# Which 64 KB block of a head's K and V each SBUF partition receives, and how the load's source is written

## The chip, the core and the metric

One core of a Trainium2 chip runs the whole program. The core has compute engines with their own instruction queues (PE for matmuls, DVE for vector work, ACT for activations, POOL, and SP, which here only issues transfers) and 16 DMA engines that move data between the device memory (HBM) and the on-chip memory SBUF, which has 128 partitions. The metric is the device time of one execution in microseconds. The kernel before took 354.75 us (median of 3 runs, 354.65 to 355.23).

## The reference

One decoding step of a transformer block for a single token of width 512. A conditioning vector gives six modulation vectors; a layer norm and a projection give 32 query heads of 128; each group of four query heads attends to one of 8 cached key/value heads with 32,768 positions; then come the output projection, a residual, a second layer norm and a small feed-forward part.

```
mod = (silu(c) @ w_mod)                       # 512 x 3072
h = layernorm(x) * (1 + ca) + sa
q = h @ wq                                    # 32 heads of 128
scores = einsum(q, k_cache) * 128 ** -0.5     # 8 kv heads, 32768 positions each
p = softmax(scores)
o = einsum(p, v_cache)
x = x + ga * (o @ wo)
h = layernorm(x) * (1 + cb) + sb
x = x + gb * (relu(h @ w1) @ w2)
```

All arrays are bfloat16. One head's K is 32,768 x 128 x 2 bytes = 8 MB, and so is its V; the 8 heads make 134.2 MB, beside 15.2 MB of weights. The sum over positions doesn't depend on their order, as long as K and V of a head use the same one.

## The kernel before, in words

The kernel streams everything once. A head's K is seen as 128 blocks of 256 consecutive positions; a block is 64 KB of consecutive bytes (256 positions x 128 values x 2 bytes) and goes to one partition. The views `kv` and `vv` (L63, L64) say which: partition p receives block p, for K and V alike.

```
    kv = A_k_cache[0].rearrange("g (p j) d -> g p j d", p=P)
    vv = A_v_cache[0].rearrange("g (p j) d -> g p j d", p=P)
```

**Loads.** `load` (L108 on) makes one transfer out of a key such as `("k", g, steps)`: `steps` names quarters of the head, each with 64 positions per partition (`TK = 64`). A whole head in one transfer is 128 rows of 64 KB (8192 KB), two steps are 128 rows of 32 KB (4096 KB) with one row starting 64 KB after the other in HBM, and one step is 128 rows of 16 KB. The destination is a tile of the pool `ring`, which has three slots of 64 KB per partition. `stream_dma` (L140, L141) issues the transfer on SP's queue. Every large load of the program goes through this one line, in the order of the list `stream`: half of K of head 0, w_mod, wq, the other half, then K of head g+1 and V of head g in turn, for the first heads whole, for the later ones in halves, V of the last head as a half and two quarters, and at the end wo, w1 and w2. SP waits ahead of an issue until the slot to be filled has been read for the last time. The transfers that have been issued stand in line at the DMA engines.

**Compute.** For each head the DVE transposes K in place in 32x32 blocks (L426), PE forms the scores of all positions with four query heads (L445), the softmax follows with the exponential on ACT (L482), and PE multiplies the probabilities with V (L507), in hardware loops for the first heads. PE and DVE follow an order that is written out by hand (`manual_schedule`); K of head g+1 is turned and scored ahead of V of head g. Behind the last head come the projection with wo (L582 and its neighbours), the second layer norm, w1, w2 and one small store.

A transfer fills all its rows before its reader is released: a reader waits for the whole transfer, never for a row.

## Time and profile before

| what | value |
|---|---|
| median of 3 runs | 354.75 us |
| the profiled execution's own time | 354.43 us |
| its span from the first to the last instruction | 352.5 us |
| PE busy | 276.4 us (78%) |
| DVE busy | 200.9 us (57%) |
| HBM read | 149.42 MB, 424 GB/s over the span |
| mean granted clock of PE | 0.921 |

The profile's page lists busy times, then the span in 40 slices with the DMA engines' busy share and the GB/s that they moved, the DMA queues, the chain of work that ended last, the costliest groups of instructions and the transfers by line. A "packet" is one row's piece that one DMA engine moves. A second view, busy time by stretch, gives for any stretch of the span each engine's busy time, the granted clock, the DMA engines' mean busy share and the GB/s. A packet is counted where it ends or begins, so that short stretches can show a share a little over or under what was moved, and the ratio of GB/s to share is the steadier figure.

### The profile page before, as it was taken

To read this page: it belongs to the slowest core of one execution; us is meant where nothing else is said; L and a number is where in the kernel's file an instruction comes from. 1 tells how busy PE (TensorE), PEld (TensorE's weight loads), DVE (VectorE), ACT (ScalarE), POOL (GpSimd) and SP (SyncE) were. 2 spreads that over 40 slices of the span, in tenths; PEclk is the share of its full clock that TensorE was granted. 3 is DMA by queue.
4 is the path that set the end of the run, shared out by engine and by line. 5 is a ranking of instruction groups with operands and counts; after the bars stand their busy time and mean duration, and the time that the engine had idled before them with its cause. 6 is when DMAs were issued, how large, how long until landed. Compare 5 with 4: busy or idle time off the path is not lost. (4 is left out here: it accounts for less than half of the span.)

```text
span 352.5 us, 3650 instructions
## 1 busy us (share of the span) xinstructions
PE 276.4 (78%) x1285; PEld 112.7 (32%) x1285; DVE 200.9 (57%) x226; ACT 25.1 (7%) x69; POOL 3.1 (1%) x15
## 2 busy tenths in 40 slices
PE   0055891995998599976998499867999789989976
PEld 0021330341333233422433233322444334434433
DVE  6662464984079613974099506975684357744142
ACT  1200103002000200001000200011000100011000
POOL 2000000000000000000000000000000000000000
PEclk9996897698999969996999989996999999999986
DMA  8999989989999999899899899999999999999995
GB/s 353 404 436 440 496 372 469 461 379 469 431 409 455 424 424 461 387 448 469 387 454 469 387 455 461 396 402 450 435 422 424 450 429 420 433 454 403 429 413 217
DMA packets 5379, 149.58 MB, mean 424 GB/s; under 512 B 632, under 2 KB 888, under 8 KB 1784
## 3 DMA queue, kind: packets, MB, share of 16 engines
q1 hardware_dynamic: 5336, 149.43, 98.5%
q8 instruction: 8, 0.13, 0.1%
q14 instruction: 3, 0.02, 0.0%
q10 hardware_dynamic: 32, 0.00, 0.0%
HBM read 149.42 MB, written 0.00 MB: 424 GB/s over the span
## 5 line engine op out<-in xcount | busy, mean ns | idle before, releaser
L426 DVE STREAM_TRANSPOSE Ksb<-Ksb 128x2048 f32<-128x2048 f32 x60 | 133.1, 2275 | 59.6 <-DMA Ksb<-in_A_k_cache_dram 59.6
L507 PE MATMUL o_ps<-Vsb,P_g 128*16 (+1 forms) x512 | 126.6, 405 | 13.3 <-ACT P_g L482 10.0
L445 PE MATMUL S_ps<-Ksb,qbd 128*128 128x512 bf16 x512 | 120.8, 388 | 10.4 <-DVE Ksb L426 8.7
L445 PEld LDWEIGHTS <-qbd 128*128 128x128 bf16 x512 | 49.8, 99 | 77.7 <-issue 21.8
L507 PEld LDWEIGHTS o_ps<-Vsb,P_g 128*16 x352 | 33.6, 95 | 68.2 <-issue 38.3
L507 PEld LDWEIGHTS <-P_g 128*16 128x16 bf16 x160 | 13.8, 90 | 19.0 <-issue 0.4
L407 ACT COPY qbd<-qrep_sb 32x16 bf16<-32x16 bf16 x32 | 6.4, 201 | 175.2 <-PE S_ps L445 174.0
L487 DVE STREAM_TRANSPOSE P_g<-P_g 128x1024 bf16<-128x1024 bf16 x8 | 10.0, 1245 | 14.1 <-ACT P_g L482 14.1
L458 DVE TENSOR_REDUCE m_p<-S_ps 128x1 f32<-128x1024 f32 x7 | 8.6, 1223 | 12.7 <-PE S_ps L445 12.7
L309 PE MATMUL mod_ps<-wmq_sb,siluT 128*1 128x512 bf16 x24 | 3.6, 623 | 9.9 <-DMA wmq_sb<-in_w_mod_dram 9.9
L318 DVE STREAM_TRANSPOSE Ksb<-Ksb 128x2048 f32<-128x2048 f32 x4 | 8.9, 2280 | 1.7 <-DMA Ksb<-in_A_k_cache_dram 1.7
L463 PE MATMUL mT_ps<-ident_f,m_p 128*1 128x128 f32 x8 | 2.2, 270 | 8.9 <-DVE m_p L458 7.9
L482 ACT ACTIVATE P_g<-S_ps,nbias 128x1024 bf16<-128x1024 f32 x8 | 8.9, 1114 | 0.2
L493 PE MATMUL L_ps<-Lexp,ones_f 128*128 128x4 f32 x16 | 3.1, 263 | 6.4 <-DVE Lexp L490 4.3
L496 DVE RECIPROCAL Linv<-L_ps 128x4 f32<-128x4 f32 x8 | 1.3, 164 | 11.7 <-PE L_ps L493 11.7
L479 ACT ACTIVATE nbias<-Mb_ps 128x1 f32<-128x1 f32 x8 | 1.4, 171 | 88.1 <-PE Mb_ps L477 88.1
L542 PE MATMUL acc_ps<-mask_sb,Y 16*128 16x4 f32 x16 | 3.1, 258 | 5.5 <-DVE Y L538 5.5
L239 PE MATMUL xc_ps<-cx_sel,wmq_sb 16*128 16x2 bf16 x4 | 0.3, 172 | 8.8 <-DVE wmq_sb L233 8.8
L535 DVE TENSOR_TENSOR o_ps<-o_ps,smask 16x512 f32<-16x512 f32 x8 | 5.3, 668 | 2.8 <-PE o_ps L507 2.8
L573 DVE CAST o_sb<-o_ps 128x4 bf16<-128x4 f32 (+2 forms) x4 | 0.7, 166 | 9.9 <-PE o_ps L569 9.9
L493 PEld LDWEIGHTS L_ps<-Lexp,ones_f 128*128 128x128 f32 x16 | 2.6, 203 | 9.7 <-issue 6.4
L538 DVE TENSOR_REDUCE Y<-o_ps 16x128 f32<-16x512 f32 x8 | 5.4, 679 | 0.3
(116 smaller groups left out, 80.6 us busy)
## 6 DMA issues: line engine op xcount, KB each, us to landing
Ksb<-in_A_k_cache_dram SPq DMA_DIRECT2D x6, 4096.0 KB, 30.3
Vsb<-in_A_v_cache_dram SPq DMA_DIRECT2D x5, 4096.0 KB, 29.5
wmq_sb<-in_A_wq_dram SPq DMA_DIRECT2D x1, 4096.0 KB, 28.1
Vsb<-in_A_v_cache_dram SPq DMA_DIRECT2D x2, 2048.0 KB, 35.5
wmq_sb<-in_w_mod_dram SPq DMA_DIRECT2D x1, 3072.0 KB, 18.9
tail_sb<-in_A_wo_dram SPq DMA_DIRECT2D x1, 2048.0 KB, 22.7
tail_sb<-in_B_w_dram SPq DMA_DIRECT2D x1, 1344.0 KB
tail_sb<-in_A_wo_dram SPq DMA_DIRECT2D x1, 1024.0 KB, 24.8
```

The source lines that it names most:

```text
L309: nc.tensor.matmul(dst[j // 4][32 * (j % 4):32 * (j % 4) + 1, :], lhsT=src_T[:, kt:kt + 1], rhs=w[:, kt, j * 512:(j + 1) * 512], start=(kt ...
L318: nc.vector.transpose(out=t, in_=t)
L407: nc.scalar.copy(out=o, in_=i)
L426: t = nc.vector.transpose(out=KTt.bitcast(F32), in_=KTt.bitcast(F32))
L445: nc.tensor.matmul(S_ps_tiles[g], lhsT=qbd[g % 2][:, hp, 4 * (7 - s):4 * (7 - s) + P], rhs=KTv[:, 16 * sl:16 * sl + 16, h, :, par], start= ...
L458: behind_loop(nc.vector.reduce_max(out=m_p[:], in_=S_g.rearrange("p g f -> p (g f)"), axis=AX.X))
L482: nc.scalar.activation(out=P_g[:], in_=S_g.rearrange("p g f -> p (g f)"), func=ACT.Exp, bias=nbias[:], scale=scale, accum_out=l_g[:],)
L487: behind_loop(nc.vector.transpose(out=P_g[:], in_=P_g[:]))
L493: nc.tensor.matmul(L_ps[:], lhsT=ones_f[:], rhs=Lexp[:], start=True, stop=True)
L507: nc.tensor.matmul(o_tiles[g][:], lhsT=PT, rhs=Vx, start=False, stop=False, skip_group_check=True)
L535: nc.vector.tensor_tensor(out=o, in0=o, in1=smask[:].unsqueeze(2).to_broadcast([16, 4, Dh]), op=ALU.mult,)
L538: nc.vector.tensor_reduce(out=Y[:], in_=o.rearrange("p s d -> p d s"), op=ALU.add, axis=AX.X)
```

## The change

The views of K and V are cut in another way, and the load flattens each row. A head's 128 blocks are numbered by two indices, block = 16 i + e with e from 0 to 15 and i from 0 to 7, and the source is written with e outermost: 16 groups, 1 block apart, of 8 rows, 16 blocks (1 MB) apart, of consecutive bytes. The destination is as before: 128 partitions in order, each with one row. Read in order, the row (e, i) of the source goes to partition 8 e + i. So partition 8 e + i holds block 16 i + e, where it held block 8 e + i. K and V use the same order, the sizes of rows and transfers, their number, their order and every compute instruction stay as they are, and so do the loads of the weights.

```
-    kv = A_k_cache[0].rearrange("g (p j) d -> g p j d", p=P)
-    vv = A_v_cache[0].rearrange("g (p j) d -> g p j d", p=P)
+    kv = A_k_cache[0].rearrange("g (i e j) d -> g e i j d", e=16, i=8)
+    vv = A_v_cache[0].rearrange("g (i e j) d -> g e i j d", e=16, i=8)
...
             g, steps = key[1], key[2]
-            src = (kv if kind == "k" else vv)[g, :, TK * steps[0]:TK * (steps[-1] + 1), :]
+            src = (kv if kind == "k" else vv)[g, :, :, TK * steps[0]:TK * (steps[-1] + 1), :]
+            src = src.rearrange("e i j d -> e i (j d)")
             name = f"Ksb{g}" if kind == "k" else f"Vsb{g}"
             t = piece(name, TK * Dh * steps[0], TK * Dh * len(steps)).rearrange("p (j d) -> p j d", d=Dh)
```

## The prediction

> **What bounds the kernel now.** I read the page's first three parts, then the chain, then busy time by stretch, then the transfers and SP's waits.

> ```profile
> span 352.5 us, 3650 instructions
> ...
> PE 276.4 (78%) x1285; PEld 112.7 (32%) x1285; DVE 200.9 (57%) x226; ACT 25.1 (7%) x69; POOL 3.1 (1%) x15
> ...
> DMA  8999989989999999899899899999999999999995
> ...
> DMA packets 5379, 149.58 MB, mean 424 GB/s; under 512 B 632, under 2 KB 888, under 8 KB 1784
> ...
> q1 hardware_dynamic: 5336, 149.43, 98.5%
> ...
> DMA 10%; PE 5%; DVE 2%; issue 0%; SPq 0%
> DMA tail_sb<-in_A_wo_dram 7%; DMA tail_sb<-in_B_w_dram 3%; PE S_ps L445 3%; PE o_ps L507 2%; DVE Ksb L426 1%; PE end_ps L767 0%; DVE Y L538 0%; DVE o_ps L535 0%; PE acc_ps L542 0%; PE L_ps L493 0%; SPq L141 0%; DVE o_rows L772 0%; DVE o_bf L774 0%; DVE Linv L496 0%; PE o_ps L569 0%
> ```

> SP's queue keeps the 16 DMA engines occupied for 98.5% of the span, while PE has 78%. The chain covers only the last 17% and is mostly transfers, so it doesn't carry the argument. The stretches do:

> ```profile
> core 0: us, PE busy (x) PEld busy (x) DVE busy (x) ACT busy (x) POOL busy (x), PEclk, DMA share, GB/s
> 1.80:12.00 10.20, 0.85 (x6) 0.79 (x7) 6.25 (x30) 2.59 (x3) 1.35 (x5) 1.00 0.98 404
> 12.00:20.00 8.00, 0.00 (x0) 0.00 (x0) 7.14 (x4) 0.35 (x2) 0.00 (x0) 1.00 1.06 456
> 20.00:29.00 9.00, 5.68 (x34) 2.30 (x34) 4.55 (x13) 0.84 (x2) 0.00 (x0) 0.89 0.96 415
> 40.00:230.00 190.00, 155.96 (x642) 62.54 (x641) 117.50 (x90) 12.19 (x36) 0.00 (x0) 0.92 1.00 434
> 320.00:334.00 14.00, 14.00 (x67) 5.83 (x65) 2.98 (x8) 0.00 (x0) 0.00 (x0) 1.00 0.98 417
> 334.00:349.20 15.20, 12.44 (x139) 6.05 (x138) 5.45 (x22) 0.76 (x3) 0.00 (x0) 0.78 0.96 395
> ```

> From 40 to 230 us whole heads stream in 64 KB rows: share 1.00, 434 GB/s, so 434 / 16 = 27.1 GB/s per engine, or 65,536 B / 27.1 GB/s = 2.42 us per row. The stretches at 12 and 20 us are w_mod and wq, whose rows lie back to back in HBM and are 24 and 32 KB long (3 MB and 4 MB over 128 rows); GB/s over share is 430 and 432 there. The rate is one constant, whatever the row's length from 24 to 64 KB and whatever the distance between neighbouring rows. It is a fixed width, not HBM's mood, and every engine has all of it. PE is busy for 156.0 of 190 us: compute waits for data.

> ```profile
> Ksb<-in_A_k_cache_dram SPq DMA_DIRECT2D x6, 4096.0 KB, 30.3
> Vsb<-in_A_v_cache_dram SPq DMA_DIRECT2D x5, 4096.0 KB, 29.5
> ...
> Vsb<-in_A_v_cache_dram SPq DMA_DIRECT2D x2, 2048.0 KB, 35.5
> ...
> Ksb<-in_A_k_cache_dram SPq DMA_DIRECT2D x5, 35.9
> Vsb<-in_A_v_cache_dram SPq DMA_DIRECT2D x5, 38.4
> ```

> ```profile
> DVE Ksb L426 <- DMA Ksb<-in_A_k_cache_dram: 59.6, 8, 13.1
> ```

> The last two transfer rows are the ten whole heads (8192 KB each, by the kernel). K and V together are 10 x 8192 + 11 x 4096 + 2 x 2048 KB = 131,072 KB = 134.2 MB; at 433 GB/s (just under the 434 of the long stretch) that is 310 us of the 352.5.

> **The change, part by part.** *Instructions.* None is added or removed on any compute engine: zero. The order of positions is the same for K and V, and each reader waits for a whole transfer, so no new wait arises in the program. *Issues on SP.* 23 loads of K and V are described in another way, with 16 groups of 8 rows.

> ```profile
> L141 SPq DMA_DIRECT2D Ksb<-in_A_k_cache_dram x11: 327/328/532, 0.7 to 271.6; - x11
> ...
> SPq L141 <- PEq L512: 124.8, 6, 21.9
> SPq L141 <- DVE Ksb L426: 124.3, 8, 25.1
> ```

> If each issue takes 532 ns (the longest here) and not 328, SP spends 23 x 0.2 = 4.7 us more; SP's waits of 124.8 and 124.3 us hide it, except ahead of the very first load: at most 0.2 us. Behind SP's issues stand only other loads and the final store.

> *The reading side.* Sixteen engines read blocks 64 KB apart at one time and step by 1 MB. Each row stays 64, 32 or 16 KB of consecutive bytes. Bounds by rows: nothing to gain, because every engine already has its constant width; the price of a bad pattern is bounded by the slowest bulk stretch, 395 GB/s at 334 us (small rows): 134.2 MB at 395 is 340 us, so +30 us. I take 0, by the rows at 12, 20 and 40 us, which differ in spacing and not in rate. [...]

> *The writing side.* This decides. Today both sides of a load are 128 rows, and the hardware may deal them to 16 engines in any order that suits SBUF. After the change the source's outer count is 16 and the destination's is 128. The only cut into sixteenths that both descriptions have in common is one group e per engine: engine e writes partitions 8e to 8e+7 one after another. At row i, engines e and e+4 then write partitions 8e+i and 8e+32+i, always 32 apart. If partitions 32 apart hang on one entrance to SBUF as wide as one engine's stream, the pair shares 27.1 GB/s: a 64 KB row takes 4.84 us and not 2.42, and only half the entrances work at a time. No row of the trace shows such a meeting, so its cost is bounded by 0 (the constant is each engine's own width and the entrances are wider) and by the whole time of K and V once more, +310 us (the constant is the entrance's). I take the upper end, less a correction: the constant is the same to 1% at three row lengths and with all HBM patterns, which is what a port on the receiving side would give, and an in-step pair has nothing that parts it.

> [...]

> *The correction.* Pairs aren't started exactly together. The first stretch moved 404 where 433 would be full: 10.2 x (1 - 404/433) = 0.7 us is the most that the start is spread; I take 0.2 us between two of a pair. Each time that the leader passes to its next four partitions, the two are apart for that long. Whole heads have 10 x 2 such passages, halves and quarters 13 x 2, together 46 x 0.2 = 9 us, say 10.

> *The sum.* 354.4 + 310 - 10 = 654 us. It is made against the profiled execution (354.43, of which 352.5 is the span); the median of 354.75 lies 0.3 above, which is nothing here. What is late next: every transpose of K waits for its load (59.6 us now, up to 310 more); PE's 156 us of work per 190 us of stream fits twice into the doubled stretch, so nothing new becomes the bound. The weights' loads keep their form; w_mod only arrives later, behind the doubled first half (4 MB, 9.7 us more, inside the 310).

> **The rivals.** *The pairs fall out of step (slower, but far less).* If one of a pair gets more than half of the entrance, it moves ahead until it writes its second four partitions while the other writes its first, and they never meet again. For: nothing makes the shares exactly equal. Against: an even share keeps any lead as it is. Price: being four rows late once, 4 x 2.42 = 9.7 us. At the first half heads four rows take half as long, a lead of 9.7 us is then a whole round and the pair meets again: another 4.8 us if it parts again (369 us in all), or all halves and quarters doubled, 11 x 4096 + 2 x 2048 KB = 50.3 MB, 116 us (480 us). I take 400.

> *The cut stays as it is (not slower).* The hardware deals destination partitions as before and finds each one's source, or engines are not hindered by a shared entrance. Then only the reading side changes, which I priced at 0: 354.4 us. What decides is whether a 64 KB row still takes 2.42 us. For: the destination is unchanged and the 27.1 may be an engine's own width. Against: the two sides no longer have an outer count in common.

> *Reading costs something (slightly slower).* The cut stays, but 16 streams 64 KB apart get in each other's way in HBM: up to +30 us by the row at 334 us; half of that is 369 us.

> *Reading gains.* Neighbouring blocks are served faster. The most that a share of 1.00 leaves is the ends: 354.4 down to some 353.5. Against it stands the constant 27.1.

> **How the numbers follow.** Pairs meet throughout: 0.45 (own range 610 to 668 us: a larger correction of 50 us, and none, plus a few us of small costs). Pairs fall out of step: 0.19. The cut stays, no change: 0.21. Reading costs: 0.11. Reading gains: 0.04. About 0.2% is what a measurement can tell here, so slower has 0.45 + 0.19 + 0.11 = 0.75, same 0.21, faster 0.04. The prediction is the likeliest, 654. Since no single neighbour of it brings 8 in 10, the range runs from no change, 354, to 668; it leaves out the gain and the few per cent above.

> **What would show it.** If pairs meet: packets stay at 5379, the DMA share stays near 1.00 in the long stretch (a packet counts while it is held up) and GB/s there is about 217 and not 434; landings of whole heads go from 35.9 us to about 75; the weights' stretches keep 430 over share; DVE's wait at L426 grows by some 300 us. If pairs part: the slices show 217 only in the first one or two loads, and again where the halves begin. If the cut stays: 434 throughout. The prediction is wrong if a row of K keeps its 2.42 us.

## The result, and the profile after

The changed kernel takes 686.18 us (median of 6 runs, 679.55 to 688.75) where the kernel before takes 354.7 us (median of 6, 354.5 to 355.23): 1.931 times as long, with a 95% interval of 1.9215 to 1.9405. That is 331 us more. It lies 18 us above the upper end of the predicted range. The profiled execution took 679.55 us, its span 677.6 us.

The head of the page of the changed kernel, with the slices of the DMA engines' share and of the GB/s:

```profile
span 677.6 us, 3650 instructions
...
PE 306.4 (45%) x1285; PEld 121.0 (18%) x1285; DVE 201.0 (30%) x226; ACT 25.1 (4%) x69; POOL 3.1 (0%) x15
...
DMA  9999998999989989989999999998999999999997
GB/s 195 362 279 218 240 193 186 244 190 193 240 187 232 201 186 236 198 186 240 193 205 224 190 232 201 187 232 191 213 205 214 217 209 215 223 230 219 226 306 292
DMA packets 5379, 149.58 MB, mean 221 GB/s; under 512 B 632, under 2 KB 888, under 8 KB 1784
...
q1 hardware_dynamic: 5336, 149.43, 99.1%
```

The packets are the same in number, size and bytes, the engines are as occupied as before (99.1% beside 98.5%), and they move half as much (221 GB/s over the span beside 424). The two higher slices early hold w_mod and wq, whose loads weren't changed: from 28 to 37 us the stream runs at 431 GB/s, at a share of 1.00.

Busy time by stretch of the changed kernel (the last columns are granted clock, DMA share and GB/s):

```profile
40.00:230.00 190.00, 81.03 (x324) 31.41 (x324) 58.30 (x47) 9.87 (x32) 0.00 (x0) 0.69 1.01 210
230.00:440.00 210.00, 91.28 (x367) 36.22 (x365) 61.73 (x47) 4.36 (x14) 0.00 (x0) 0.72 1.00 207
440.00:640.00 200.00, 98.77 (x360) 37.98 (x359) 55.15 (x57) 6.22 (x14) 0.47 (x1) 0.74 1.00 215
```

210 and 207 GB/s stand where 434 stood. Per engine that is 13.1 and 12.9 GB/s: a row of 64 KB takes about 5.0 us and not 2.42. The trace also keeps the duration of each single row, which no view prints: the 1,280 rows of 64 KB take 2.42 us before and 5.09 us after (medians), and the shortest after takes 4.83. Who waits is what was expected; here are the transfers, DVE's wait and SP's issues:

```profile
Ksb<-in_A_k_cache_dram SPq DMA_DIRECT2D x5, 102.7
Vsb<-in_A_v_cache_dram SPq DMA_DIRECT2D x5, 101.5
```

```profile
DVE Ksb L427 <- DMA Ksb<-in_A_k_cache_dram: 349.1, 10, 55.1
```

```profile
L142 SPq DMA_DIRECT2D Vsb<-in_A_v_cache_dram x12: 536/537/600, 45.8 to 554.8; - x12
L142 SPq DMA_DIRECT2D Ksb<-in_A_k_cache_dram x11: 536/537/669, 0.7 to 516.1; - x11
```

DVE's wait for K grew from 59.6 to 349.1 us. Each issue of K and V costs SP 537 ns and not 328, which is hidden as before. The landing of a whole head takes 102.7 us, because a load is still issued as soon as its slot has been read: its own 8192 KB take 40 us at 210 GB/s, and for the rest of the time it stands behind one and a half others.

### The profile page after: what moved, and what is told of

Its sections match the earlier page's. It is cut to its first block, busy times and chain, and to the rows that moved or that the text cites. A ratio compares the mean times of both kernels' runs of the same rounds, so it can differ in the third digit from the quotient of the medians.

```text
span 677.6 us, 3650 instructions
## 1 busy us (share of the span) xinstructions
PE 306.4 (45%) x1285; PEld 121.0 (18%) x1285; DVE 201.0 (30%) x226; ACT 25.1 (4%) x69; POOL 3.1 (0%) x15
## 2 busy tenths in 40 slices
DMA packets 5379, 149.58 MB, mean 221 GB/s; under 512 B 632, under 2 KB 888, under 8 KB 1784
## 3 DMA queue, kind: packets, MB, share of 16 engines
q1 hardware_dynamic: 5336, 149.43, 99.1%
## 4 chain that ended last, share of the span: by engine, by line
another core or an unknown queue 55%; DVE 22%; PE 14%; DMA 6%; ACT 2%; issue 1%; SPq 0%; DVEq 0%; ACTq 0%
DVE Ksb L427 17%; PE S_ps L446 6%; PE o_ps L508 6%; DMA wmq_sb<-in_A_wq_dram 6%; ACT P_g L483 1%; DVE m_p L459 1%; DVE P_g L488 1%; DVE Y L539 1%; DVE o_ps L536 1%; PE q_ps L381 1%; PE end_ps L768 0%; DVE o_ps L528 0%; PE acc_ps L543 0%; PE hid_ps L745 0%
## 5 line engine op out<-in xcount | busy, mean ns | idle before, releaser
L427 DVE STREAM_TRANSPOSE Ksb<-Ksb 128x2048 f32<-128x2048 f32 x60 | 133.1, 2277 | 349.1 <-DMA Ksb<-in_A_k_cache_dram 349.1
L446 PE MATMUL S_ps<-Ksb,qbd 128*128 128x512 bf16 x512 | 137.8, 430 | 169.6 <-DVE Ksb L427 168.1
L508 PE MATMUL o_ps<-Vsb,P_g 128*16 (+1 forms) x512 | 139.0, 435 | 138.7 <-issue 104.6
L446 PEld LDWEIGHTS <-qbd 128*128 128x128 bf16 x512 | 53.6, 106 | 250.1 <-DVE Ksb L427 110.9
L508 PEld LDWEIGHTS <-P_g 128*16 128x16 bf16 x160 | 16.5, 105 | 61.6 <-issue 50.2
L467 DVE TENSOR_REDUCE Mrow<-mT_ps 1x4 f32<-1x128 f32 x8 | 2.2, 274 | 15.8 <-PE mT_ps L464 15.8
L381 PE MATMUL q_ps<-wmq_sb,hT 128*1 128x512 bf16 x32 | 3.4, 598 | 2.5 <-DMA wmq_sb<-in_A_wq_dram 2.5
## 6 DMA issues: line engine op xcount, KB each, us to landing
Ksb<-in_A_k_cache_dram SPq DMA_DIRECT2D x6, 4096.0 KB, 80.4
Vsb<-in_A_v_cache_dram SPq DMA_DIRECT2D x5, 4096.0 KB, 82.4
wmq_sb<-in_A_wq_dram SPq DMA_DIRECT2D x1, 4096.0 KB, 38.3
Vsb<-in_A_v_cache_dram SPq DMA_DIRECT2D x2, 2048.0 KB, 92.1
tail_sb<-in_A_wo_dram SPq DMA_DIRECT2D x1, 2048.0 KB, 47.8
```

The costliest lines, as they stand in the source:

```text
L381: nc.tensor.matmul(q_ps[i][32 * a:32 * a + 1, :].rearrange("o (h e) -> o h e", e=32), lhsT=hT[:, kt:kt + 1], rhs=wq_f[:, kt, i, a], start= ...
L427: t = nc.vector.transpose(out=KTt.bitcast(F32), in_=KTt.bitcast(F32))
L446: nc.tensor.matmul(S_ps_tiles[g], lhsT=qbd[g % 2][:, hp, 4 * (7 - s):4 * (7 - s) + P], rhs=KTv[:, 16 * sl:16 * sl + 16, h, :, par], start= ...
L508: nc.tensor.matmul(o_tiles[g][:], lhsT=PT, rhs=Vx, start=False, stop=False, skip_group_check=True)
```

## The experiments

Four theories were held against each other. **W**, the prediction's: the new source is cut so that one engine writes eight consecutive partitions, engines e and e+4 write 32 partitions apart in step, and partitions 32 apart share one entrance, so that the two that meet are slow. **R**: the new order of reads in HBM is slow. **D**: a source of three dimensions is slow in itself. **F**: an engine is slow when it writes partitions that the plain 128-row load gives to another engine. Two more, **C** and **S**, came up on the way.

**The old neighbourhoods, cut as after.**

```
-    kv = A_k_cache[0].rearrange("g (i e j) d -> g e i j d", e=16, i=8)
+    kv = A_k_cache[0].rearrange("g (e i j) d -> g e i j d", e=16, i=8)
...
+            (se, ne), (si, ni), row = src.ap
+            src = AP(src.tensor, src.offset + (ni - 1) * si, [[se, ne], [-si, ni], row])
```

(V likewise. The step backwards is only there to keep the source from being read as 128 equal rows.)

> K and V are again read in the old neighbourhoods (partition 8e+7-i gets... block 8e+7-i is read as row i of group e, so engine e reads the same eight neighbouring blocks as the natural order has), but the source is written as 16 groups of 8 rows with a step backwards, so that it can't be read as 128 equal rows. Every K and V byte is read once, K and V in the same order. Theory W (the cut into 16 groups makes two engines write through one entrance of SBUF, in step): as slow as the changed kernel, 675 to 690 us, about 210 GB/s in the long stretch. Theory R (reading blocks 64 KB apart with steps of 1 MB is slow in HBM): like the kernel before, 354 to 360 us and 434 GB/s. Theory D (a source of three dimensions is slow for the DMA engines in itself): 675 to 690 us, as W.

Measured: 686.64 us (680.06 to 688.04), 1.9276 times the kernel before (1.9174 to 1.9379). Its long stretch:

```profile
40.00:230.00 190.00, 77.45 (x315) 30.17 (x315) 58.30 (x47) 9.87 (x32) 0.00 (x0) 0.71 1.00 207
```

The whole loss is there without the new order of reads. R falls, W and D stand.

**Reads 64 KB apart, cut as before.**

```
+            src = src.rearrange("p j d -> p (j d)")
+            src = AP(src.tensor, src.offset, [[TK * Dh, P], src.ap[1]])
```

This kernel leaves out most of K and V: its rows overlap.

> The source stays 128 equal rows, but rows start 16 KB apart and overlap, so that rows four apart lie 64 KB apart and several engines read in neighbouring 64 KB; most of K and V isn't read, and parts are read up to four times. The same bytes per transfer, the same destination. Theory W: like the kernel before, 354 to 356 us, 434 GB/s. Theory R: clearly slower, as far as 686 us if 64 KB between neighbours is the cause. Theory D: 354 to 356 us.

Measured: 354.84 us, 0.9996 times the kernel before (0.9986 to 1.0005), and at full width:

```profile
40.00:230.00 190.00, 155.23 (x642) 62.24 (x641) 117.12 (x90) 12.18 (x36) 0.00 (x0) 0.92 1.00 432
```

R falls from this side too.

**Groups of four rows in place of eight.**

```
-    kv = A_k_cache[0].rearrange("g (i e j) d -> g e i j d", e=16, i=8)
+    kv = A_k_cache[0].rearrange("g (i e j) d -> g e i j d", e=32, i=4)
```

(V likewise.)

> The source is cut into 32 groups of 4 rows (block = 32 i + f, group f from 0 to 31, row i from 0 to 3, partition 4 f + i): again three dimensions that can't be read as 128 equal rows, again neighbouring groups 64 KB apart and rows 2 MB apart, every byte read once. What differs from the changed kernel is that a group is four partitions and not eight. Theory W (which partitions one engine writes decides): if the hardware can deal groups of four to engines as it deals single rows, 354 to 357 us and 434 GB/s. Theory D (a source of three dimensions is slow in itself): 675 to 690 us and 210 GB/s. Theory R (reads 64 KB apart) would also say 675 to 690, but the run with rows 16 KB apart already speaks against it.

Measured: 354.88 us, ratio 1.0 (0.9991 to 1.001).

```profile
40.00:230.00 190.00, 155.49 (x639) 62.31 (x638) 116.50 (x90) 12.19 (x36) 0.00 (x0) 0.92 1.00 431
```

D falls: three dimensions cost nothing here (431 GB/s beside 434), where a group is four partitions. That groups of four go to the engines as single rows do is inferred from the unchanged rate. The idea of the change, engines reading near each other, neither gains nor loses anything in this run, as the prediction priced it.

**The entrances, one row at a time.** Ahead of the kernel before, ten small loads five times over, each with rows of 64 KB, one per engine (eight per engine in the last), to chosen partitions. Between them stands a load of 128 short rows, which makes each wait for the one before. (In the code cuts from here on, words behind a # are the document's.)

```
+        quiet()
+        nc.sync.dma_start(out=onto(0, 4, 4), in_=some[0:4])     # first partition, count, step
```

> The kernel before, with small loads ahead of it, one after another, five times each, into the slot that K of head 1 fills later: rows of 64 KB, one per engine, to chosen partitions; each waits for the one before. The time from issue to landing of each form, beside a fixed part common to all. (1) partitions 0,1,2,3; (2) 0,4,8,12; (3) 16,20,24,28; (4) 0,8,16,24; (5) 0,32,64,96; (6) 0,4,...,28; (7) 0,8,...,56; (8) 0,8,...,120; (9) 0,4,...,60; (10) all 128. Theory W: a row takes 2.4 us where every engine has its own entrance, (2), (3), (4) and (6); 4.8 us where two meet, (5), (7), (8) and (9), so 2.4 us more than (2); 9.7 us for (1). Theory F: (3) and (4) are as slow as (7) though no two engines meet. Theory D says nothing here: all have two dimensions.

SP's lines for four probes of the fourth round, in order of time. L174 is the load between; the time from a probe's start to the start of the next L174 is its time from issue to landing, with a part common to all. The table has nine; the tenth, all 128 rows, took 21.67 us. Rounds two to five agree within 0.25 us, and the first is disturbed by the kernel's own first loads.

```profile
337.88 0.27 SPq L179 DMA_DIRECT2D Ksb<-in_A_k_cache_dram  x1
348.79 0.33 SPq L174 DMA_DIRECT2D Ksb<-in_A_k_cache_dram  x1
350.54 0.65 SPq L181 DMA_DIRECT2D Ksb<-in_A_k_cache_dram  x1
355.78 0.33 SPq L174 DMA_DIRECT2D Ksb<-in_A_k_cache_dram  x1
...
372.00 0.55 SPq L187 DMA_DIRECT2D Ksb<-in_A_k_cache_dram  x1
379.14 0.33 SPq L174 DMA_DIRECT2D Ksb<-in_A_k_cache_dram  x1
...
396.93 0.56 SPq L193 DMA_DIRECT2D Ksb<-in_A_k_cache_dram  x1
404.68 0.33 SPq L174 DMA_DIRECT2D Ksb<-in_A_k_cache_dram  x1
```

| line | partitions | us to landing |
|---|---|---|
| L179 | 0, 1, 2, 3 | 10.91 |
| L181 | 0, 4, 8, 12 | 5.24 |
| L183 | 16, 20, 24, 28 | 5.25 |
| L185 | 0, 8, 16, 24 | 5.24 |
| L187 | 0, 32, 64, 96 | 7.14 |
| L189 | 0, 4, ..., 28 | 5.08 |
| L191 | 0, 8, ..., 56 | 7.26 |
| L193 | 0, 8, ..., 120 | 7.75 |
| L195 | 0, 4, ..., 60 | 7.60 |

**Pairs shifted against each other.** If a meeting slows only its pair, shifting one of each pair by its four rows should end the loss in the whole heads. Three extra loads of 64 KB rows to partitions 0–11, 0–7 and 0–3 are meant to occupy the lower engines first (which engine serves which row isn't shown); the second kernel has rows of 32 KB.

```
+    late = NTILE * TK * Dh        # the second kernel: // 2
+    for k in (12, 8, 4):
+        nc.sync.dma_start(out=piece("Ksb1", 0, late)[0:k], in_=kv[0].rearrange("e i j d -> e i (j d)")[0:k, 0, 0:late])
```

> The changed kernel, with three small extra loads at the start: 64 KB rows to partitions 0 to 11, 0 to 7 and 0 to 3 of the slot that K of head 1 fills later. They occupy engines 0 to 11, 0 to 7 and 0 to 3, four engines on one entrance, so each takes about four rows' time (9.7 us) and engines 0-3 come to lag 4-7, and 8-11 to lag 12-15, by four rows of a whole head. Theory W: the pairs no longer meet in the whole heads (434 GB/s there, from about 60 us on), and meet again in the halves, where 9.7 us is a whole round (about 210 GB/s): some 510 us in all, 480 to 540. Theories R and D: nothing gained, 686 + 29 = 715 us, 210 GB/s in the whole heads.

> The same with extra loads of 32 KB rows, so that the lag is 4.85 us. Theory W, with a lag that stays as it is: in the whole heads a pair meets for half of the time (each four rows take 1.5 times as long, 275 to 290 GB/s), and in the halves, whose four rows take 4.85 us, the pairs no longer meet (434 GB/s): the reverse of the run with the full lag; some 475 us in all, 455 to 500. Theories R and D: 686 + 15 = 700 us, 210 GB/s throughout.

Measured: 694.67 us (2 runs, 692.04 to 697.29) and 703.14 us (2 runs). The whole heads of the first kernel and a stretch that has mostly its halves, then the whole heads of the second:

```profile
100.00:230.00 130.00, 53.34 (x207) 21.05 (x206) 43.08 (x31) 5.65 (x15) 0.00 (x0) 0.70 1.00 209
440.00:640.00 200.00, 104.06 (x383) 40.28 (x384) 67.82 (x59) 5.29 (x14) 0.47 (x1) 0.74 1.00 231
```

```profile
100.00:230.00 130.00, 52.56 (x200) 20.50 (x200) 44.05 (x33) 4.36 (x14) 0.00 (x0) 0.70 1.00 209
```

No gain in the whole heads, and none in the time, against what W expected. So W lacked something, or eight consecutive partitions per engine are slow for a reason of their own (theory S).

**A cut into seven consecutive partitions.** The order of the kernel before, with each load in two.

```
+            stream_dma(t[0:112], src[0:112])
+            stream_dma(t[112:P], src[112:P])
```

> The order of the kernel before, with two dimensions on both sides, but each load of K and V in two: partitions 0 to 111 and partitions 112 to 127. 112 isn't cut like 128: seven consecutive partitions per engine. If only two engines that stand on the same entrance at one moment slow each other (Theory W in the form of the prediction, entrances repeating after 32 partitions), few of the 112 rows meet: 7 rows of 2.42 us, and the 16 rows, four engines to an entrance, 9.7 us: 26.6 us per 8 MB and not 19.3, 310 us become some 430, in all 460 to 500 us. If any engine that writes other partitions than those dealt to it in the 128-row load is slow (Theory F, foreign entrances): 7 x 4.84 + 9.7 = 43.5 us per 8 MB, in all some 740 us. Theory D: as the first, 460 to 500 us.

Measured: 699.37 us (2 runs, 697.62 to 701.11); its long stretches:

```profile
40.00:230.00 190.00, 82.87 (x330) 32.30 (x323) 58.29 (x47) 9.87 (x32) 0.00 (x0) 0.69 1.01 215
230.00:440.00 210.00, 90.72 (x358) 35.67 (x357) 60.90 (x46) 4.36 (x14) 0.00 (x0) 0.71 1.01 213
440.00:640.00 200.00, 91.40 (x334) 34.93 (x333) 52.66 (x52) 5.36 (x14) 0.47 (x1) 0.71 0.99 200
```

Counted so, and if each engine takes seven consecutive partitions, the 16 engines stand on 14 or 15 different entrances at each row of the larger load, so only one or two pairs meet; still all of it runs at half pace (200 to 215 GB/s). With F unlikely after the probes, this and the two runs before suggest theory C: **a shared entrance sets the pace of all sixteen engines.** Taken strictly, C gives 7 x 4.84 + 9.7 = 43.5 us per 8 MB, or 193 GB/s, and W gives 26.6 us, or 315 GB/s; the 200 to 215 measured lie nearer to C, and the difference is open. By C the shifts of the two kernels before didn't become what was meant either. While the lower engines filled a crowded entrance, the leaders were held to the same pace, and their lead in the end was the bytes of one extra row (64 KB, one row and not four). Pairs one row apart still meet in three rows of four, and as the two sets of pairs are shifted by two rows against each other, there is no moment of the whole heads without a meeting. In the halves a lead of 64 KB is two rows: there all pairs are apart in two rows of four, and all meet in the other two. From 500 to 640 us the first kernel does move 238 to 242 GB/s, where the changed kernel has 218 and the second one 212. An estimate from the row times (1.21 us before, 2.56 us in the control below) would be 278, so C gives the direction of this gain and not its size. All of this was worked out after these runs.

**All pairs apart, or half of them.** Theory C says how to get rid of the loss: make leads in bytes, and for all pairs at once. Loads in halves throughout make four rows 128 KB; one extra load of 24 rows is meant to give engines 0–11 128 KB more, and two of 4 rows to give engines 0–3 another 128 KB.

```
-        stream += [("k", g + 1, s) for s in (halves if g >= HALVED else whole)] + [("v", g, s) for s in (halves if g >= HALVED else whole)]
+        stream += [("k", g + 1, s) for s in halves] + [("v", g, s) for s in halves]
...
+    later = piece("Ksb1", 0, NTILE * TK * Dh)
+    lp = later.ap[0][0]
+    extra = [(24, 0, 1), (4, 24, 4), (4, 25, 4)]      # rows, first partition, step; the second kernel: the first alone
+    for n, first, step in extra:
+        to = AP(later.tensor, later.offset + first * lp, [[step * lp, n], [1, NTILE * TK * Dh]])
+        nc.sync.dma_start(out=to, in_=A_k_cache[0, 0].rearrange("(p j) d -> p (j d)", p=P)[0:n])
```

> The changed kernel with all loads of K and V in halves (rows of 32 KB, so that four rows are 128 KB per engine), and three extra loads behind the first: 24 rows of 64 KB (engines 0 to 11, 128 KB each) and twice 4 rows of 64 KB (engines 0 to 3, 128 KB). Engines 12-15 then lead 8-11 by 128 KB, and 4-7 lead 0-3 by 128 KB: both sets of pairs are apart by exactly four rows. Theory C (one entrance that two engines share sets the pace of all sixteen, so only a schedule without any meeting is fast; bytes moved, not time, make a lead): no meeting is left in the halves, 400 to 434 GB/s in the long stretch, 375 to 430 us in all. Theory W in the form of the prediction (a pair's meeting slows that pair only): the same. Theory S (a load that is cut into eight consecutive partitions per engine is slow whatever the order in time): 690 to 705 us and 210 GB/s.

> The same with only the first extra load (24 rows, engines 0 to 11): engines 12-15 lead 8-11 by four rows, and 0-3 stay in step with 4-7. Theory C: the meetings that are left slow all sixteen engines, 210 GB/s at a DMA share of 1.00, 685 to 700 us, no gain from half of the meetings being gone. Theory W in the form of the prediction: engines 8 to 15 move their rows at full pace and stand idle until the others are done, so about the same time and GB/s, but a DMA share of about 0.75. Theory S: share 1.00, 690 us.

> The changed kernel with all loads of K and V in halves and no extra load: the control of the two others. All theories: as the changed kernel, 675 to 695 us, 205 to 217 GB/s.

Measured: all pairs apart 440.6 us (436.25 to 443.43), 1.2447 times the kernel before (1.2401 to 1.2493), above the 375 to 430 us expected; half of them apart 660.87 and 691.77 us (two executions); the control 676.77 us (2 runs), 1.9077 (1.9039 to 1.9116). Three stretches with all pairs apart:

```profile
120.00:180.00 60.00, 46.30 (x192) 18.08 (x191) 31.34 (x28) 4.36 (x14) 0.00 (x0) 0.91 1.00 406
180.00:240.00 60.00, 48.92 (x211) 20.26 (x209) 36.53 (x27) 2.60 (x10) 0.00 (x0) 0.89 1.01 401
360.00:420.00 60.00, 38.03 (x165) 14.65 (x163) 16.86 (x23) 2.66 (x4) 0.47 (x1) 0.83 0.99 293
```

and two with half of the pairs apart (of the execution of 691.77 us; the other left no trace):

```profile
120.00:230.00 110.00, 45.51 (x167) 17.46 (x165) 32.26 (x28) 4.36 (x14) 0.00 (x0) 0.69 1.00 210
230.00:440.00 210.00, 98.81 (x373) 38.10 (x374) 59.75 (x46) 4.36 (x14) 0.00 (x0) 0.74 1.01 212
```

and one of the control:

```profile
40.00:230.00 190.00, 85.43 (x325) 32.73 (x325) 58.52 (x47) 9.87 (x32) 0.00 (x0) 0.71 1.00 208
```

The same cut into eight consecutive partitions runs at 401 to 406 GB/s (208 in the control) with the extra loads that are to keep any two engines from one entrance at a time, so S falls, and with it F: the loads of K and V, and so the partitions that an engine writes, are those of the control. The stretch from 360 us has the two quarters of the last V, in whose shorter rows a lead of 128 KB is a whole round; there the rate drops again, as it should: two slices of the page, 10.9 us each, have 210 and 213 GB/s from 380 us on.

With half of the pairs apart the trace has the rate of the control, and the share is 1.00 and not 0.75. The single rows settle who is slow: from 60 to 440 us none of the 2,442 rows of 32 KB takes less than 2.16 us, and their median is 2.56, as in the control; with all pairs apart it is 1.27 (120 to 300 us), and before it was 1.21. If only the pairs that meet were slow, half of the rows would be near 1.21. So, if the first extra load parts the pairs that it is meant to part, the engines that meet nobody are as slow as the others. That is theory C, and it speaks against pairs that slow only themselves. By the same count four entrances are shared at every moment of this kernel; that a single one would do the same isn't shown. The two executions lie 5% apart: the shorter one is 16 us under the control and under the 685 to 700 that C expected, so a gain of some 2% from half of the pairs isn't excluded.

Of the 86 us by which the first kernel misses the kernel before, some 26 are lost ahead of 60 us, 9 from there to 120, 18 from 120 to 360 and 19 from 360 to 420 us (an estimate from each stretch's GB/s against 433). The 2.1 MB of the extra loads are another 5 us. The rest wasn't taken apart, nor why 401 to 406 GB/s aren't 434.

## Why the prediction was right or wrong

- **What bounds the kernel** held: DMA at a constant 27.1 GB/s per engine, and compute that waits. Nothing new became the bound.
- **The reading side at 0** held: ratios of 0.9996 and 1.0 with reads 64 KB apart, and the same time with the new order of reads (686.18 us) and the old one (686.64 us) under the same cut.
- **Issues on SP** held: 537 ns beside the 532 ns that the text took, all hidden.
- **The writing side**, the mechanism that decided, held: an engine's eight consecutive partitions, pairs 32 apart, one entrance for two. Where it fell short is in who is slowed: not only the pair, but all sixteen engines, as the run with half of the pairs apart indicates (no row of 32 KB under 2.16 us). In the changed kernel every pair meets, so rows come out about doubled either way (5.09 us beside 2.42). The run with the old read order shows that the cut alone brings the loss, the probes show the entrances, the groups of four show that the cut is what matters, and the run with all pairs apart that the meeting does it. That engine e gets exactly partitions 8e to 8e+7 is inferred from these, not read off a trace, and so are the engines that the extra loads occupy and the reason given for the dealing, the outer counts of 16 and 128.
- **Its size was wrong**, and with it the range: 686.18 us lies above 668. Two terms of the sum failed. The upper end of "+310 us, the whole time of K and V once more" was taken as a bound, but two engines on one entrance together move less than one alone: at 210.6 GB/s (the mean of the three stretches after, weighted by their length) K and V take 134.2 / 210.6 = 637 us, 327 more and not 310 (a row took 5.09 us, not 4.84). And **the correction of 10 us was worth nothing.** It let each pair gain from its own small offset, once for every four partitions, and no run shows such a gain: in the runs with shifted pairs (209 GB/s in the whole heads) a pair's offset is worth nothing, or next to nothing, while other pairs meet. That four neighbouring partitions share an entrance, which the correction and the rival below both count with, was an assumption that no row of the trace before shows; the probes show it for partitions 0 to 3 (10.91 us, where 0, 4, 8 and 12 took 5.24). With both terms put right, 354.4 + 327 = 681 us beside the 679.55 of the profiled execution, the shortest of the six. The 210.6 is read from that same execution, so the sum says that no third term is missing, and not why the rate is what it is.
- **The rival "pairs fall out of step"** rested on the same wrong step. Pairs can be out of step, as in the two runs with extra loads, and the loss stays whole in the whole heads; only when all are apart at once does most of it go.
- **What would show it:** the packets, the share, 217 GB/s (210 came) and DVE's wait (289.5 us more, some 300 said) were as told, and the weights kept their rate. The landing was not: 102.7 us, not 75. A whole head's own 19 us became 40, but its waiting in line grew from some 17 to some 63 us (the landing less its own time), since slots come free earlier against the slower stream.

## What to carry to other kernels

In these runs a load's rate hung on which partitions were written at one time. 128 rows against 128, and groups of four partitions, kept the full rate (434 and 431 GB/s); groups of eight cost a factor of 1.93 in time (210 GB/s) though every byte, row and packet was the same, and loads cut into 112 and 16 partitions were as slow (699.37 us). That the outermost counts of the two sides settle the dealing is the prediction's inference; only these forms were tried. The sign in this profile was a DMA share of 1.00 at half of the usual GB/s. Don't price a contended entrance only by the engines that stand on it: with half of the pairs apart the whole stream moved 210 GB/s here, as with none apart (208).

## What was not expected of the hardware

**Crowded entrances held up all sixteen engines.** With half of the pairs apart: 210 GB/s at share 1.00, and no row of 32 KB under 2.16 us; with all of them apart, 401 to 406 GB/s. How an engine that meets nobody comes to be held up isn't shown.

**Two on one entrance moved less than one alone, in a long stream.** If every pair meets after the change, eight entrances carry the 207 to 210 GB/s of the whole heads, 25.9 to 26.3 each, where one engine alone had 27.1 before (434 / 16). In the probes, with one row per engine, it isn't so: four rows of 64 KB on one entrance run in 8.4 to 9.2 us from the first start to the last end, 29 to 31 GB/s. So the loss belongs to the long stream. Why wasn't tried.

**PE's clock was lower where PE waited more.** It was granted 0.733 of full speed after (0.921 before), with PE busy for 45% of the span (78% before), and 0.888 with all pairs apart, where PE was busy for 65%; the score matmuls (L445 before, L446 after) took 430 ns on average and not 388. What lowers the clock wasn't tried. It costs nothing here, since PE waits for data.
